# Joined input loads, sixteen rows of batch 5 loaded apart, and wide fp32 idle products in a linear-attention and soft-MoE kernel

## The chip, the core and the metric

The kernel runs on one core of one Trainium2 chip. Five engines work at the same time, each through its own list of instructions: TensorE (PE; its weight loads are listed apart as PEld), VectorE (DVE), ScalarE (ACT), GpSimd (POOL) and SyncE (SP). Here SP only issues the transfers between HBM and SBUF, which 16 DMA engines carry out. The metric is the device time of one execution in microseconds (us).

## The reference

Linear attention over 8 batches and 8 heads of 576 tokens of 64 features is followed by a root-mean-square norm; the result, 4608 tokens of 512 features, goes through a soft mixture of 8 experts with 4 slots each:

```python
kv = einsum('bhsd,bhse->bhde', k, v)
out = einsum('bhsd,bhde->bhse', q, kv)
x = out / sqrt(mean(out * out) + 1e-6) * g_norm      # 4608 x 512
logits = x @ phi                                     # 4608 x 32
d = softmax of logits over the 4608 tokens
slot_input = d.T @ x                                 # 8 experts x 4 slots x 512
slot_out = relu(slot_input @ w1[e]) @ w2[e]          # w1 512 x 1024, w2 1024 x 512
c = softmax of logits over the 32 slots
result = c @ slot_out                                # 4608 x 512
```

All data is fp32.

## The kernel before

The 4608 tokens are 36 tiles T of 128 tokens. Nine tiles make two batches.

**Attention.** For each batch b the class `Kv` builds the products of k and v in PSUM, for 8 heads at once. `products` (L205) multiplies the first 512 tokens, in four blocks of 128 rows for each of four head groups. `borders` (L220) adds the last 64 tokens. They lie in `kv_rest`, for one half of the batch (`g`) and one `w` on partitions 0 to 63, for the other `w` on partitions 64 to 127; the two halves of the output (`i`) go to rows 0 to 63 and 64 to 127 of PSUM, so that the four products of a half each have a quarter of PE's array. Then ACT copies the result to SBUF (`kvT`, L229), and `slots` (L234, L236) transposes it and multiplies it by phi; ACT and DVE put the results into one of two block-diagonal operands `bd` (L240, L248, L250). `kv_steps` says before which tile the steps (0, 1 and 2) of a batch run.

**Tiles.** For each T, `products(T)` (L264, L273) multiplies q by `bd` into a PSUM tile `o`, of which there are two; ACT squares it and evicts it (L283, L290, L291), DVE sums the squares (L296), ACT and DVE make the root (L304 to L314), POOL scales (L345, L323), DVE makes logits (L358), and every six tiles a running maximum and PE's `group_sum` (L422) add to the slot inputs `acc`.

**Experts.** After the last tile, `expert_h(e)` (L637) multiplies slot inputs by w1 and `expert_y(e, hf)` (L655) by w2, for two halves hf of the output columns. Half 0 of experts 2 to 7 runs through units 2, 3 and 4 of w2, two experts in each unit; half 1 runs through units 5, 6 and 7. `gather` and `mix` (L671, L675, L677) finish a half, and `output` (L688, L696, L698) makes one twelfth of the result and, when a row of `OUT_ROWS` is complete, sends it (L702).

**Idle products.** `fill(n)` (L465) issues n bf16 matmuls of zeros, 512 columns wide, whose result nobody reads. `EARLY` sets how many stand ahead of the first products and behind each half of batch 0, `LATE_FILL` how many stand at five places between the last tile and the experts.

**Transfers.** All of them are issued by SP, in the program's order. A load whose home is still being read waits, and what is behind it in SP's list waits with it. `place` addresses a large SBUF arena in units of 256 columns, whose parts are used again and again: `KV_AT`, `Q_AT`, `W_AT` and `OUT_AT` say where. `W_ROWS` lists the loads of weights, each the parts of one row next to each other. `loads_behind` says behind which tile a load is issued. Before the change, w2's units 3 and 4 are two loads, the first issued behind `expert_h(0)`, the second behind `expert_h(1)`.

Of the kernel before, what the change touches and what calls it, by code (L numbers as in the profile page):

```python
# [8 lines left out]
F32 = mybir.dt.float32  # L9
# [5 lines left out]
P = 128  # L15
# [12 lines left out]
NX = 14  # L28
EARLY = (9, 1, 0)
LATE_FILL = (16, 3, 3, 1, 1)  # L30
TOK = 4608
# [6 lines left out]
W_AT = {  # L38
# [3 lines left out]
}  # L42
W_ROWS = (
    (("w1", 0, None), ("w2", 0, None)),
    (("w1", 1, None), ("w2", 1, None)),
    (("w1", 2, None), ("w1", 3, None)),
    (("w1", 4, None), ("w2", 2, 1)),
    (("w1", 5, None),),
    (("w1", 6, None),),
    (("w1", 7, None),),  # L50
    (("w2", 2, 0),),
    (("w2", 3, None),),
    (("w2", 4, None),),
    (("w2", 5, None),),
# [4 lines left out]
OUT_ROWS = ((0, 1), (2, 3), (4, 5), (6,), (7, 8), (9, 10, 11))  # L59
HEAD = 144  # L60
SCRATCH = 1024
EPS_RMS = 1e-6
# [7 lines left out]
@with_exitstack  # L70
def soft_moe_linear_attention(ctx: ExitStack, tc: tile.TileContext, first_in, head_in, t2_in, kv5_in, t3_in, w_in, out):


    nc = tc.nc
# [10 lines left out]
    def place(at, n):  # L85
        return arena[:, HEAD + at * KB : HEAD + at * KB + n]

    def load_head(u, lo, hi):
        at = (KV_AT[0], KV_AT[1], Q_AT[0], KV_AT[2], Q_AT[1], KV_AT[3])[u]
        nc.sync.dma_start(place(at, TOK)[:, lo:hi], head_in[u, :, lo:hi])  # L90

    def load_row(at, src):
        nc.sync.dma_start(place(at, src.shape[-1]), src)
# [4 lines left out]
    def kv_rest(b, g):  # L98
        return place(KV_AT[b], TOK)[:, g * 2304 + 2048 : g * 2304 + 2304]

    def q_main(b):
# [22 lines left out]
    def w_block(kind, u, i):  # L124
# [8 lines left out]
    load_head(2, 0, 2048)  # L133
    load_head(1, 0, 2304)
    load_head(1, 2304, TOK)
    load_head(2, 2048, TOK)
# [6 lines left out]
        18: lambda: load_w("w1", 0),  # L143
        21: lambda: load_w("w1", 1),
        26: lambda: load_w("w1", 2),
        27: lambda: load_w("w1", 4),
        31: lambda: load_w("w1", 5),
    }
# [5 lines left out]
    ones = const.tile([P, P], F32, name="ones")  # L154
# [11 lines left out]
    for i in range(2):  # L166
        lo = 64 * i
# [20 lines left out]
    class Kv:  # L188
# [24 lines left out]
        def borders(self, gs):  # L213

            for g in gs:
                half = kv_rest(self.b, g).rearrange("p (w n) -> p w n", w=2)
                for i in range(2):
                    for w in range(2):
                        lo, at = 64 * i, 64 * w
                        nc.tensor.matmul(  # L220
                            self.pkv[lo : lo + 64, w, g],
                            lhsT=half[at : at + 64, 1, lo : lo + 64],
                            rhs=half[at : at + 64, 0, lo : lo + 64],
                            start=False,
                            stop=g == gs[-1],
                        )
            n = len(gs)
            self.kvT = wk.tile([P, n, 2, D], F32, tag="kvT", name=f"kvT{self.b}_{gs[0]}", bufs=1)
            nc.scalar.copy(self.kvT, self.pkv[:, :, gs[0] : gs[0] + n].rearrange("p w g d -> p g w d"))  # L229
# [206 lines left out]
    kv_steps = {(b, i - 3): (i,) for b in range(2, B) for i in range(3)}  # L436
    kv_steps.update({(1, -2): (0, 1), (1, -1): (2,)})

    def kv_step(b, i):
        if i == 0:  # L440
            kvs[b] = Kv(b)
            kvs[b].products(0)
            kvs[b].products(1)
        elif i == 1:
            kvs[b].products(2)
            kvs[b].products(3)
            kvs[b].borders((0, 1))
        else:
            kvs[b].slots((0, 1))
# [9 lines left out]
    def fill(n, cols=256, home=None):  # L459
# [4 lines left out]
        for i in range(n):  # L464
# [6 lines left out]
            )  # L471

    fill(EARLY[0], cols=512)

    for g in range(2):
        kv = Kv(0, "o" if g else "kv", 2 if g else None)
        kv.products(2 * g)
        kv.products(2 * g + 1)
        kv.borders((g,))
        kv.slots((g,))  # L480
        fill(EARLY[1 + g], cols=512)
    load_head(5, 0, TOK)
    load_head(4, 2048, TOK)
    load_row(KV_AT[4], t2_in)
    load_row(KV_AT[5], kv5_in)
    T_at, diag_at, pb_at, d_at, sums_at = {}, {}, {}, {}, {}
    for T in range(NT - 2):
# [4 lines left out]
        s = ends.get(T - 1)  # L492
# [64 lines left out]
    for i in todo_sums:  # L557
        group_sum(*i)
    load_w("w1", 6)
    load_w("w1", 7)  # L560
    load_w("w2", 2, 0)
    fill(LATE_FILL[0], home=ps.tile([P, 512], F32, tag="m", name="fill"), cols=512)
    group_max_T(G)
# [141 lines left out]

    expert_h(0)
    load_w("w2", 3)
    expert_h(1)
    load_w("w2", 4)
    expert_y(0, 0)  # L710
# [38 lines left out]
def build_program():  # L749
# [3 lines left out]
    shapes = {  # L753
        "first": (P, HEAD + 2304), "head": (6, P, TOK), "t2": (P, 2 * TOK), "kv5": (P, TOK), "t3": (P, 3 * TOK),
        "w": (1, 2 * NE * P * UNIT),
# [62 lines left out]
```

## Time and profile before

| | us |
|---|---|
| time, median of 3 runs (lowest, highest) | 175.09 (174.84, 175.16) |
| the profiled execution's own time | 174.76 |
| its span, first to last instruction | 173.0 |
| PE busy | 150.3 |
| DVE busy | 89.1 |
| ACT busy | 86.4 |
| POOL busy | 57.2 |

The span leaves out 1.8 us of the execution's own time. The page says how long each engine was busy, what share of the span the DMA engines worked, and it follows back the chain of work that ended last. Times of instructions are counted from the start of the span. PE works on fp32 in two records for each matmul, so 16 matmuls appear as x32. Other views quoted below give instructions in order of time (start, length, engine, line, operation, count, and in brackets the idle time before), the busy time in stretches (length; busy time of PE, PEld, DVE, ACT and POOL, each with its count of instructions; the granted clock of PE; the busy share of the DMA engines; GB/s), and for transfers the line, size and time from issue to landing.

### The profile page before, as it was taken

How to read it: one execution, taken by the hardware profiler on the slowest of the kernel's cores; microseconds unless marked ns; L12 is line 12 of the kernel's file. 1: busy time of each engine (PE TensorE's matmuls, PEld its weight loads, DVE VectorE, ACT ScalarE, POOL GpSimd, SP SyncE). 2: the span in 40 equal slices, each digit the busy share in tenths (PEclk: the TensorE clock that was granted, in tenths of full speed). 3: DMA queues.
4: the chain of work that ended last, by engine and by line, in shares of the span. 5: the costliest groups of instructions: out<-in, count | busy, mean ns of one | idle time of the engine just before them, and what ended most of it. 6: DMA issues, size and time to landing. Idle time of an engine off the chain costs nothing.

```text
span 173.0 us, 4659 instructions
## 1 busy us (share of the span) xinstructions
PE 150.3 (87%) x1973; PEld 108.3 (63%) x1973; DVE 89.1 (51%) x184; ACT 86.4 (50%) x224; POOL 57.2 (33%) x68
## 2 busy tenths in 40 slices
PE   7788999999979899999999796989999899978500
PEld 2467978888769788888897583346666435433200
DVE  1111456566576656566664776842888433456600
ACT  2024586976947976878859465112222131315500
POOL 6000067636557753477563676600000000000000
PEclk9999999999999999999999999999999999999955
DMA  5999999999999998999999999999999999999994
GB/s 199 420 429 427 447 404 447 399 506 409 405 413 473 479 435 359 417 436 415 440 440 415 426 411 421 424 432 415 434 419 424 424 424 425 393 404 418 418 452 196
DMA packets 4628, 71.67 MB, mean 414 GB/s; under 512 B 512, under 2 KB 512, under 8 KB 640
## 3 DMA queue, kind: packets, MB, share of 16 engines
q1 hardware_dynamic: 4608, 71.38, 97.3%
q8 instruction: 15, 0.25, 0.6%
q14 instruction: 5, 0.04, 0.1%
HBM read 61.94 MB, written 9.44 MB: 413 GB/s over the span
## 4 chain that ended last, share of the span: by engine, by line
PE 54%; DVE 16%; ACT 12%; POOL 5%; issue 4%; DMA 3%; POOLq 1%; DVEq 0%; ACTq 0%
PE o L273 13%; PE pY L655 9%; PE ph L637 8%; PE kvp_kv L205 7%; PE po L688 6%; POOL part L345 4%; DVE logits L358 4%; DVE ms L296 4%; DMA arena<-in_first_dram 3%; PE pS L422 2%; ACT sq L283 2%; DVE arena L698 2%; ACT bd L240 2%; ACT xall L291 1%; ACT r L304 1%
## 5 line engine op out<-in xcount | busy, mean ns | idle before, releaser
L273 PE MATMUL o<-bd,arena 128*128 128x192 f32 x256 | 49.3, 336 | 1.6 <-ACT xall L291 0.6
L273 PEld LDWEIGHTS o<-bd,arena 128*128 128x128 f32 x256 | 41.0, 191 | 4.4 <-ACT xall L291 1.7
L345 POOL TENSOR_TENSOR part<-part,r 128x512 f32<-128x512 f32 x17 | 17.8, 1047 | 52.6 <-DVE r L314 52.6
L323 POOL TENSOR_TENSOR xall<-xall,r 128x512 f32<-128x512 f32 x34 | 34.7, 1043 | 0.0
L358 DVE TENSOR_REDUCE logits<-part 128x64 f32<-128x512 f32 (+1 forms) x18 | 18.3, 1014 | 16.5 <-POOL part L345 16.4
L296 DVE TENSOR_REDUCE ms<-sq 128x16 f32<-128x1024 f32 (+1 forms) x19 | 21.9, 1154 | 5.8 <-ACT sq L283 5.7
L283 ACT ACTIVATE sq<-o 128x512 f32<-128x512 f32 x36 | 21.4, 596 | 6.1 <-PE o L273 5.8
L291 ACT COPY xall<-o 128x512 f32<-128x512 f32 x34 | 20.7, 609 | 0.0
L205 PE MATMUL kvp_kv<-arena 128*64 128x64 f32 x480 | 17.9, 231 | 0.9 <-DMA arena<-in_first_dram 0.9
L205 PEld LDWEIGHTS kvp_kv<-arena 128*64 128x64 f32 x480 | 15.9, 144 | 4.3 <-issue 1.9
L696 ACT COPY arena<-po 128x768 f32<-128x768 f32 x12 | 9.3, 800 | 18.5 <-PE po L688 18.4
L698 DVE COPY arena<-po 128x768 f32<-128x768 f32 x12 | 11.3, 956 | 10.6 <-PE po L688 9.8
L655 PE MATMUL pY<-arena,xall 128*32 128x256 f32 x256 | 15.6, 382 | 0.5 <-DVE y L671 0.5
L688 PE MATMUL po<-logits,z 32*128 32x384 f32 x96 | 13.5, 525 | 2.1 <-DVE z L677 0.9
L637 PE MATMUL ph<-arena,sTe 128*32 128x256 f32 x224 | 12.7, 380 | 0.3 <-DVE sTe L584 0.3
L655 PEld LDWEIGHTS pY<-arena,xall 128*32 128x32 f32 x256 | 7.8, 110 | 7.8 <-issue 1.4
L290 ACT COPY part<-o 128x256 f32<-128x256 f32 x34 | 12.6, 372 | 0.0
L304 ACT ACTIVATE r<-ms,eps 128x16 f32<-128x16 f32 x17 | 5.2, 308 | 14.7 <-DVE ms L296 14.5
L422 PE MATMUL pS<-xall,d 128*32 128x129 f32 x288 | 10.8, 278 | 2.0 <-ACT d L410 2.0
L688 PEld LDWEIGHTS po<-logits,z 32*128 32x128 f32 x96 | 5.8, 183 | 8.9 <-ACT arena L696 5.0
L637 PEld LDWEIGHTS ph<-arena,sTe 128*32 128x32 f32 x224 | 7.2, 110 | 5.3 <-DVE sTe L584 0.7
L422 PEld LDWEIGHTS pS<-xall,d 128*32 128x32 f32 x288 | 7.1, 109 | 5.1 <-issue 4.2
(93 smaller groups left out, 143.9 us busy)
## 6 DMA issues: line engine op xcount, KB each, us to landing
arena<-in_w_dram SPq DMA_DIRECT2D x7, 2048.0 KB, 17.6
arena<-in_w_dram SPq DMA_DIRECT2D x3, 4096.0 KB, 22.9
arena<-in_t_dram SPq DMA_DIRECT2D x1, 6912.0 KB, 36.1
out_dram<-arena SPq DMA_DIRECT2D x4, 1536.0 KB, 7.2
arena<-in_head_dram SPq DMA_DIRECT2D x2, 2304.0 KB, 22.5
arena<-in_t_dram SPq DMA_DIRECT2D x1, 4608.0 KB, 35.3
arena<-in_head_dram SPq DMA_DIRECT2D x3, 1152.0 KB, 11.9
arena<-in_w_dram SPq DMA_DIRECT2D x1, 3072.0 KB, 26.0
```

Source lines behind the costliest of these rows:

```text
L205: nc.tensor.matmul(self.pkv[lo : lo + 64, w, g], lhsT=main[:, w, 1, c, lo : lo + 64], rhs=main[:, w, 0, c, lo : lo + 64], start=c == 0 and ...
L273: nc.tensor.matmul(o[:, r, :192], lhsT=q_main(2 * g + i)[:, r, at : at + P], rhs=bds[i][:, r], start=True, stop=True)
L283: nc.scalar.activation(sqs[s][:, T - starts[s]], o[:, :, 32:160], AF.Square, scale=0.125)
L291: nc.scalar.copy(xts[T % NX][:, :, :128], o[:, :, 32:160])
L296: nc.vector.tensor_reduce(out=mss[s], in_=sqs.pop(s).rearrange("p t j (w d) -> p (t j w) d", w=2), axis=AX.X, op=ALU.add)
L323: nc.gpsimd.tensor_tensor(out=x, in0=x, in1=r[:, i].rearrange("p (j w) -> p j w", w=2).unsqueeze(3).to_broadcast([P, 4, 2, D]), op=ALU.mult,)
L345: engine.tensor_tensor(out=part, in0=part, in1=rs_of[s].unsqueeze(3).to_broadcast([P, STAGES[s], H, NS]), op=ALU.mult)
L358: nc.vector.tensor_reduce(out=L[:, pos(starts[s]) : pos(starts[s]) + STAGES[s]], in_=parts.pop(s).rearrange("p t h n -> p t n h"), axis=AX ...
L422: nc.tensor.matmul(pS[32 * j : 32 * j + 32], lhsT=ds[G][:, i], rhs=x[:, j], start=i == 0, stop=i == GROUPS[G] - 1)
L637: nc.tensor.matmul(ph[32 * j : 32 * j + 32], lhsT=sTe[:, (4 * e + c) * NS : (4 * e + c + 1) * NS], rhs=w_block("w1", e, 4 * c + j), start= ...
L655: nc.tensor.matmul(pY[32 * j : 32 * j + 32, hf, :256], lhsT=hTs[e][:, c], rhs=w_block("w2", u, at + c), start=e == 0 and c < 4, stop=e == ...
L688: nc.tensor.matmul(po[:, u, : CT * NS].rearrange("p (g x) -> p g x", g=2), lhsT=z[lo : lo + 32, f * P : (f + 1) * P], rhs=cT[k][lo : lo + 32],
```

## The change

Four things change; the rest of the diff follows from them.

1. **Loads joined.** k and v of batch 1 come in one load in place of two, and all three steps of batch 1 now run before tile 3 (before: steps 0 and 1 before tile 2, step 2 before tile 3). In `W_ROWS`, half a unit of w2 (`("w2", 2, 0)`), w1 of expert 6 and w1 of expert 5 become one load of 5 MB, issued behind the last tile; w2's units 3 and 4 become one load of 4 MB, issued behind `expert_h(1)`. The first two rows of weights are paired otherwise, with the same sizes and places.
2. **Batch 5.** The last 64 tokens of half 1 of batch 5 no longer ride on that batch's load (each of its 128 rows is 256 columns, 1 KB, shorter). They come as 16 rows of 2048 columns, in four transfers of four rows (rows i, i+4, i+8, i+12), issued between the loads of batch 4 and batch 5. `borders` multiplies them in 16 products of 16 rows in place of 4 products of 64 rows. All 16 stand on partitions 0 to 15.
3. **Wide idle products.** `fill_wide(n)` issues n fp32 matmuls of ones, 128 by 512 columns. Two stand behind the bf16 ones at the start, one each ahead of batches 1 and 2, and four take the place of the 16 bf16 ones behind the last tile.
4. **bf16 idle products.** At the start there are 5 in place of 9, and one more stands between `borders` and `slots` of each half of batch 0.

```diff
-EARLY = (9, 1, 0)
-LATE_FILL = (16, 3, 3, 1, 1)
+EARLY = (5, 1, 0)
+WIDE = (2, 1, 1)
+LATE_FILL = (4, 3, 3, 1, 1)
...
-    (("w1", 5, None),),
-    (("w1", 6, None),),
+    (("w2", 2, 0), ("w1", 6, None), ("w1", 5, None)),
     (("w1", 7, None),),
-    (("w2", 2, 0),),
-    (("w2", 3, None),),
-    (("w2", 4, None),),
+    (("w2", 3, None), ("w2", 4, None)),
...
+    def rest_pieces(b, g, w, cols):
+        if (b, g) == APART:
+            t = place(APART_AT, 2048)[:APART_ROWS].rearrange("p (s w c n) -> p s w c n", w=2, c=2, n=128)
+            return [(t[:, s, w, 1, cols], t[:, s, w, 0, cols]) for s in range(64 // APART_ROWS)]
+        t = kv_rest(b, g)[64 * w : 64 * w + 64].rearrange("p (c n) -> p c n", c=2)
+        return [(t[:, 1, cols], t[:, 0, cols])]
...
-    load_head(1, 0, 2304)
-    load_head(1, 2304, TOK)
+    load_head(1, 0, TOK)
...
-        31: lambda: load_w("w1", 5),
...
+                        pieces = rest_pieces(self.b, g, w, slice(64 * i, 64 * i + 64))
+                        for n, (v, k) in enumerate(pieces):
+                            nc.tensor.matmul(
...
-    kv_steps.update({(1, -2): (0, 1), (1, -1): (2,)})
+    kv_steps[1, -1] = (0, 1, 2)
...
         if i == 0:
+            if b < 3:
+                fill_wide(WIDE[b])
...
+    def fill_wide(n):
+        t = ps.tile([P, 512], F32, tag="m", name="fill").rearrange("p (a n) -> p a n", n=P)
+        for i in range(n):
+            nc.tensor.matmul(t, lhsT=ones, rhs=ones.unsqueeze(1).to_broadcast([P, 4, P]), start=True, stop=True)
+
     fill(EARLY[0], cols=512)
+    fill_wide(WIDE[0])
...
         kv.borders((g,))
+        fill(1, cols=512)
         kv.slots((g,))
...
     load_row(KV_AT[4], t2_in)
+    rest = place(APART_AT, 2048)[:APART_ROWS]
+    for i in range(4):
+        nc.sync.dma_start(rest[i::4], rest_in[i::4])
     load_row(KV_AT[5], kv5_in)
...
-    load_w("w1", 6)
+    load_w("w2", 2, 0)
     load_w("w1", 7)
-    load_w("w2", 2, 0)
...
     expert_h(0)
+    expert_h(1)
     load_w("w2", 3)
-    expert_h(1)
-    load_w("w2", 4)
     expert_y(0, 0)
```

Three places show what stands where. The first is PE around batch 1, before the change: kvp_kv and kvp_o are the products of k and v, o the tiles, kvT and gphi the operands of `slots`.

```order
L205 MATMUL kvp_o<-arena 64x64 x16
L220 MATMUL kvp_o<-arena 64x64 x4
L234 MATMUL kvp_o<-ident,kvT_1_167 128x128
L236 MATMUL kvp_o<-gphi,kvT_1_167 128x128
L273 MATMUL o_179<-bd_93,arena 128x192 x4
L273 MATMUL o_189<-bd_93,arena 128x192 x4
L205 MATMUL kvp_kv<-arena 64x64 x32
L220 MATMUL kvp_kv<-arena 64x64 x8
L273 MATMUL o_242<-bd_93,arena 128x192 x4
L234 MATMUL kvp_kv<-ident,kvT_0_240 128x128 x2
L236 MATMUL kvp_kv<-gphi,kvT_0_240 128x128 x2
```

The same place after the change:

```order
L242 MATMUL kvp_o<-gphi,kvT_1_167 128x128
L279 MATMUL o_185<-bd_92,arena 128x192 x4
L279 MATMUL o_195<-bd_92,arena 128x192 x4
L279 MATMUL o_205<-bd_92,arena 128x192 x4
L484 MATMUL fill<-ones 128x512
L211 MATMUL kvp_kv<-arena 64x64 x32
L226 MATMUL kvp_kv<-arena 64x64 x8
L240 MATMUL kvp_kv<-ident,kvT_0_269 128x128 x2
L242 MATMUL kvp_kv<-gphi,kvT_0_269 128x128 x2
L279 MATMUL o_279<-bd_92,arena 128x192 x4
```

The third tile's products moved ahead of batch 1, a wide idle product stands between, and no tile stands any more between the borders of batch 1 and its slots.

The second place is PE around the borders of batch 5, before and after; pS is `group_sum`, pm the maximum.

```order
L422 MATMUL pS_743<-xall,d_712 32x129 x8
L205 MATMUL kvp_kv<-arena 64x64 x16
L220 MATMUL kvp_kv<-arena 64x64 x8
L273 MATMUL o_818<-bd_93,arena 128x192 x4
L386 MATMUL pm_831<-ident,top_780 128x128
```

```order
L428 MATMUL pS_753<-xall,d_722 32x129 x8
L211 MATMUL kvp_kv<-arena 64x64 x16
L226 MATMUL kvp_kv<-arena 64x64 x20
L279 MATMUL o_840<-bd_92,arena 128x192 x4
L392 MATMUL pm_853<-ident,top_790 128x128
```

Eight products became twenty, at the same place of the list.

The third place is SP's list of loads, from the load of batch 3 to the last load of weights, before and after; t is batch 4 with its q (first) and batches 6 and 7 with theirs (second), kv batch 5, w weights.

```order
L90 DMA arena<-in_head_dram 128x4608
L90 DMA arena<-in_head_dram 128x2560
L93 DMA arena<-in_t_dram 128x9216
L93 DMA arena<-in_kv_dram 128x4608
L93 DMA arena<-in_t_dram 128x13824
L122 DMA arena<-in_w_dram 128x8192 x3
L122 DMA arena<-in_w_dram 128x6144
L122 DMA arena<-in_w_dram 128x4096 x2
L122 DMA xall<-in_w_dram 128x4096
L122 DMA arena<-in_w_dram 128x2048
L122 DMA arena<-in_w_dram 128x4096 x5
```

```order
L91 DMA arena<-in_head_dram 128x4608
L91 DMA arena<-in_head_dram 128x2560
L94 DMA arena<-in_t_dram 128x9216
L502 DMA arena<-in_rest_dram 4x2048 x4
L94 DMA arena<-in_kv_dram 128x4352
L94 DMA arena<-in_t_dram 128x13824
L130 DMA arena<-in_w_dram 128x8192 x3
L130 DMA arena<-in_w_dram 128x6144
L130 DMA arena<-in_w_dram 128x10240
L130 DMA xall<-in_w_dram 128x4096
L130 DMA arena<-in_w_dram 128x8192
L130 DMA arena<-in_w_dram 128x4096 x3
```

Two loads of 4096 columns and the one of 2048 became one of 10240, two of the five behind it became one of 8192, and four small transfers stand ahead of batch 5.

More of the change, by code (lines that the diff above doesn't have):

```diff
@@ L38 @@
 W_AT = {
[1 row of a table removed]
[1 row of a table added]
     ("w1", 3): (16,), ("w1", 4): (104,), ("w1", 5): (56,), ("w1", 6): (40,), ("w1", 7): None,
[1 row of a table removed]
[1 row of a table added]
 }
 W_ROWS = (
-    (("w1", 0, None), ("w2", 0, None)),
-    (("w1", 1, None), ("w2", 1, None)),
+    (("w1", 0, None), ("w1", 1, None)),
+    (("w2", 0, None), ("w2", 1, None)),
     (("w1", 2, None), ("w1", 3, None)),
     (("w1", 4, None), ("w2", 2, 1)),
-    (("w1", 5, None),),
-    (("w1", 6, None),),
+    (("w2", 2, 0), ("w1", 6, None), ("w1", 5, None)),
     (("w1", 7, None),),
-    (("w2", 2, 0),),
-    (("w2", 3, None),),
-    (("w2", 4, None),),
+    (("w2", 3, None), ("w2", 4, None)),
     (("w2", 5, None),),
@@ L60 @@
 HEAD = 144
+APART = (5, 1)
+APART_AT = 144
+APART_ROWS = 16
 SCRATCH = 1024
@@ L70, in soft_moe_linear_attention @@
 @with_exitstack
-def soft_moe_linear_attention(ctx: ExitStack, tc: tile.TileContext, first_in, head_in, t2_in, kv5_in, t3_in, w_in, out):
+def soft_moe_linear_attention(ctx: ExitStack, tc: tile.TileContext, first_in, head_in, t2_in, kv5_in, rest_in, t3_in, w_in, out):
     nc = tc.nc
@@ L143, in soft_moe_linear_attention @@
         18: lambda: load_w("w1", 0),
-        21: lambda: load_w("w1", 1),
+        21: lambda: load_w("w2", 0),
         26: lambda: load_w("w1", 2),
         27: lambda: load_w("w1", 4),
-        31: lambda: load_w("w1", 5),
     }
@@ L215, in borders @@
             for g in gs:
-                half = kv_rest(self.b, g).rearrange("p (w n) -> p w n", w=2)
                 for i in range(2):
                     for w in range(2):
[L219 to L226, printed above, removed]
+                        pieces = rest_pieces(self.b, g, w, slice(64 * i, 64 * i + 64))
+                        for n, (v, k) in enumerate(pieces):
+                            nc.tensor.matmul(
+                                self.pkv[64 * i : 64 * i + 64, w, g],
+                                lhsT=v,
+                                rhs=k,
+                                start=False,
+                                stop=g == gs[-1] and n == len(pieces) - 1,
+                            )
             n = len(gs)
@@ L558, in soft_moe_linear_attention @@
         group_sum(*i)
-    load_w("w1", 6)
+    load_w("w2", 2, 0)
     load_w("w1", 7)
-    load_w("w2", 2, 0)
-    fill(LATE_FILL[0], home=ps.tile([P, 512], F32, tag="m", name="fill"), cols=512)
+    fill_wide(LATE_FILL[0])
     group_max_T(G)
@@ L753, in build_program @@
     shapes = {
-        "first": (P, HEAD + 2304), "head": (6, P, TOK), "t2": (P, 2 * TOK), "kv5": (P, TOK), "t3": (P, 3 * TOK),
+        "first": (P, HEAD + 2304), "head": (6, P, TOK), "t2": (P, 2 * TOK), "kv5": (P, TOK - 256), "rest": (APART_ROWS, 2048), "t3": (P, 3 * TOK),
         "w": (1, 2 * NE * P * UNIT),
@@ L796 @@
     rows = [np.concatenate([w[k] for k in row], axis=1).reshape(-1) for row in W_ROWS]
+    rest = kv[5][:, TOK - 256 :].reshape(2, 64 // APART_ROWS, APART_ROWS, 256).transpose(2, 1, 0, 3)
+    rest = rest.reshape(APART_ROWS, 2048)
     first = np.zeros((P, HEAD + 2304), np.float32)
@@ L803 @@
         "in_t2_dram": np.concatenate([kv[4], qm[2]], axis=1),
-        "in_kv5_dram": kv[5],
+        "in_kv5_dram": np.ascontiguousarray(kv[5][:, : TOK - 256]),
+        "in_rest_dram": np.ascontiguousarray(rest),
         "in_t3_dram": np.concatenate([kv[6], qm[3], kv[7]], axis=1),
```

4 rows, old and new, of the table W_AT are left out of this document.

## The prediction

> **What bounds the kernel now.** I read the page's slices and DMA queues first, then the chain of waits, then short stretches at the end.
>
> ```profile
> DMA  5999999999999998999999999999999999999994
> q1 hardware_dynamic: 4608, 71.38, 97.3%
> q8 instruction: 15, 0.25, 0.6%
> PE 54%; DVE 16%; ACT 12%; POOL 5%; issue 4%; DMA 3%; POOLq 1%; DVEq 0%; ACTq 0%
> ```
>
> The DMA engines work through nearly all of the span: 97.3% of 173.0 us for 71.38 MB is 168.3 us for the 4357 KB of each engine, 38.6 ns per KB. Yet the chain that ended last is compute, over half of it PE. So two bounds lie side by side, and the question is which one sets the last transfer. The busy share of the DMA engines near the end tells it (stretch; busy times; clock, DMA share, GB/s):
>
> ```profile
> 154.00:154.50 0.50, 0.20 (x1) 0.00 (x0) 0.50 (x1) 0.41 (x1) 0.00 (x0) 1.00 0.93 393
> 154.50:155.00 0.50, 0.00 (x0) 0.00 (x0) 0.46 (x2) 0.00 (x0) 0.00 (x0) 1.00 0.64 270
> 155.00:155.50 0.50, 0.40 (x4) 0.34 (x8) 0.00 (x0) 0.00 (x0) 0.00 (x0) 1.00 0.52 221
> 155.50:156.00 0.50, 0.50 (x10) 0.39 (x4) 0.00 (x0) 0.00 (x0) 0.00 (x0) 1.00 0.99 418
> ...
> 170.00:170.50 0.50, 0.00 (x0) 0.00 (x0) 0.00 (x0) 0.00 (x0) 0.00 (x0) 0.50 0.61 258
> ...
> 171.50:172.00 0.50, 0.00 (x0) 0.00 (x0) 0.00 (x0) 0.00 (x0) 0.00 (x0) 0.50 0.01 0
> ```
>
> SP's issues and, below, times from issue to landing, in the same order (weights, then two outputs):
>
> ```profile
> 120.23 0.33 SPq L122 DMA_DIRECT2D arena<-in_w_dram  x1
> 154.70 0.33 SPq L702 DMA_DIRECT2D out_dram<-arena  x1
> 163.54 0.33 SPq L702 DMA_DIRECT2D out_dram<-arena  x1
> ```
> ```profile
> arena<-in_w_dram SPq DMA_DIRECT2D x1, 2048.0 KB, 15.3
> out_dram<-arena SPq DMA_DIRECT2D x1, 1536.0 KB, 6.5
> out_dram<-arena SPq DMA_DIRECT2D x1, 2304.0 KB, 8.6
> ```
>
> At 155.0 half of the engines have nothing to do: they wait for the third output row, issued at 154.70, and start at about 155.6, 0.9 us behind the issue. From there 1536 + 768 + 1536 + 2304 = 6144 KB are left, 384 KB an engine, 14.8 us: these engines end at 170.4, where the share falls to 0.61. The other half was never dry and ends at 171.5; their last landing, at 163.54 + 8.6 = 172.1, closes the kernel. The lag from last packet to landing is about 0.5 us. So the waiting engines land at 170.9, and compute has **1.2 us** of room: whatever delays the third output row by less is hidden by the busier engines; what delays it by more is paid.
>
> **The change part by part, loads.** The last 256 columns of batch 5 are 8 KB for each engine, 8 x 38.6 ns = 0.3 us earlier for every later load, on engines that take none of the four small transfers. Four loads fewer are 512 packets fewer; no row prices a packet apart from its bytes, so between nothing and 0.4 us; I take 0.2, since the rows give whole transfers near their bytes' price. Together the queue is 0.5 us earlier by the time of w2. Of the small transfers the trace has no like. Spread over all engines they cost nothing net; on four engines, 4 x 8 KB each, 1.2 us there; on one, 128 KB, 4.9 us. I take four, one row of each transfer per engine, since a row was one packet in all others (4608 packets are the rows and completions of 32 transfers). Half of the engines have room for 1.2 us, as 0.52 shows; if the four are among the others, w2 comes later (a rival).
>
> [...]
>
> **The joined loads of weights.** The 5 MB load waits for what its two later parts waited for, and goes out about when the first of those did; the queue then still holds the load before it. The 4 MB load is what matters. Its second half landed at 120.23 + 15.3 = 135.5; joined, both land then, less 0.5: 135.0. Who reads the first half (PE in order of time, then waits; six experts' pY, the first of which stands in the chain below)?
>
> ```profile
> 132.07 5.55 PE L655 MATMUL pY<-arena,xall 128*32 128x256 f32 x96
> ```
> ```profile
> PEld pY L655 <- DMA arena<-in_w_dram: 0.5, 1, 0.5
> ```
>
> Six experts of x16, 0.86 us each, start at 132.07; unit 3 is needed by the third, at 133.8. It would wait until 135.1, 1.3 us, and the small wait that stood before unit 4 (0.1 us on PE itself) would go: **+1.2 us** for all output, if nothing else moved.
>
> **The borders of batch 5.** The chain of waits runs through this step:
>
> ```profile
> 17.25 2.03 PE kvp_kv L205 x64
> ...
> 22.55 0.25 ACT bd L240
> ...
> 23.75 0.60 ACT sq L283
> ...
> 64.43 1.08 PE kvp_kv L205 x32
> 65.52 0.39 PE kvp_kv L220 x16
> 65.91 1.50 PE o L273 x8
> 67.41 0.22 PE pm L386 x2
> 67.63 0.58 PE pS L422 x16
> 68.20 0.37 PE kvp_kv L234 x2
> 68.57 0.45 PE kvp_kv L236 x4
> ...
> 88.99 1.51 PE o L273 x8
> ...
> 90.53 0.60 ACT sq L283
> ...
> 116.51 3.66 PE ph L637 x64
> ...
> 120.17 0.86 PE pY L655 x16
> ```
>
> From 60.7 to 90.5 the chain is PE without a gap; nothing there hides PE work. The 8 products of L220 take 0.39 us because four, each on its quarter of the array, go side by side. In the new half, 16 products have the same 16 rows and, eight by eight, the same columns, so each waits for the one ahead. What a record costs alone no row shows for this shape. Where two go side by side (L205: 64 records in 2.03 us), a place in line is 0.063 us; 32 records one by one are 2.0 us, less half of 0.39: **+1.8 us**. Bounds: at L220's pace (0.39/16 = 0.024) 0.8 - 0.2 = +0.6; with the weight load not hidden, at L234's 0.185 a record, +5.7. I take 1.8, the row nearest in shape.
>
> Behind 90.5 the chain turns to ACT, DVE and POOL, all fed by PE, and so on to the experts: all of it moves by 1.8 us. The third expert then arrives at 133.8 + 1.8 = 135.6, after the joined load: **the two delays do not add**. The output stage moves by 1.8 less the 0.1 of the wait: 1.7 us.
>
> **The start.** PE and the load of batch 1's second part:
>
> ```profile
> 1.05 4.02 PE L465 MATMUL fill<-zeros 128*128 128x512 bf16 x9 [1.05 <-DVE zeros L157]
> 6.00 1.98 PE L205 MATMUL kvp_kv<-arena 128*64 128x64 f32 x32 [0.93 <-DMA arena<-in_first_dram]
> 13.65 0.90 PE L273 MATMUL o<-bd,arena 128*128 128x192 f32 x4
> 15.06 2.19 PE L273 MATMUL o<-bd,arena 128*128 128x192 f32 x12 [0.51 <-DVE bd L248]
> ```
> ```profile
> arena<-in_head_dram SPq DMA_DIRECT2D x1, 1152.0 KB, 15.3
> ```
> ```profile
> 2.77 0.44 SPq L90 DMA_DIRECT2D arena<-in_head_dram  x1
> ```
>
> Matmuls here take 1.98 us where the same 32 records later take 1.08: PE runs at half its later pace, though its granted clock reads 1.00. Five bf16 products (0.43 each at this pace) and two wide ones (1.7 each, from eight records of 192 columns in 1.5 us, doubled) end at 6.6 instead of 5.1, and no gap of 0.93 us stands before 6.00. Batch 1's products now wait for 2.77 + 15.3 = 18.1; 2.0 us of them, borders 0.4, copy 0.4, slots 0.8 and the copies to the square of tile 3 (22.55 to 23.75 before) 1.2 end at 22.9, against 23.75 before. So if tiles 0 to 2 are done by 18.1, the start loses nothing. For that PE must come to its later pace by about 10 us. I take it so, for the unbroken stretch from 1.05 to about 8 (6.00 + 1.98), where before it broke off at 5.1. If not, tile 2 ends near 18.8, and a wide product, the later first products and the tile buffer shared with kvp_o make the start up to **2 us** late; the gain the other way is bounded by the load, under 0.8. The wide product ahead of batch 2 lies on ACT's and DVE's time until 50. I take 0 for the start.
>
> [...]
>
> Behind the last tile nothing changes: eight records of 512 columns cost what 16 bf16 products did, and PE waits for the logits there.
>
> ```profile
> 107.25 3.63 PE L465 MATMUL fill<-zeros 128*128 128x512 bf16 x16
> 111.10 0.43 PE L388 MATMUL pm<-ident,logits 128*32 128x128 f32 x8 [0.22 <-DVE logits L371]
> ```
>
> **The sum.** The third output row goes out at 154.70 + 1.7 = 156.4; the queue, 0.5 us earlier, is dry on all engines by then. They start at 157.3 and take 14.8 us and 0.5 to land: 172.6 instead of 172.1, rounded **+0.4 us**, since the old share shows the same sum to be up to 0.1 long. The profiled execution would be 175.2 (174.76 before, 0.33 under the median), the median **175.5 us**.
>
> **The rivals.** *A, the borders are cheap* (up to +1.3 of the bounds): then the joined 4 MB load decides, the output moves by 1.2 us, exactly the room: 175.1, no change. For it: L220's own pace. *B, faster:* the third row moves by less than 0.7 us, because the loads come a full microsecond earlier or PE makes up time after 138; the queue's 0.5 us then count: 174.6. Against it: PE has nothing to wait for between 138 and 154 that could give way. *C, the four rows fall on busy engines:* w2's 4 MB land 0.7 us later than before, at 136.2, the third expert waits until 136.3, the output moves by 2.4 us: 172.1 + 1.2, so 176.3. *D, the start stays slow, or weight loads are not hidden in the borders:* 2 to 4 us more on the chain, 177.5 or above.
>
> **How the numbers follow.** Forecast 0.44, A 0.25, B 0.10, C 0.10, D 0.11. The range takes in B and C and leaves out D and the far end: 174.5 to 176.5; the forecast's own is 175.2 to 175.9. A measurement of this kernel tells 0.2%, 0.35 us, from no change. The forecast is slower by more than that in some 0.65 of its cases, C and D always: 0.29 + 0.21 = 0.50. Faster is B and a little of A: 0.13. The rest, 0.37, is the same.
>
> **What would show it.** The borders of batch 5 near 65 us should take about 2.2 us; first PE products of the experts should start 1.8 us later than 116.5 us; PE should not wait for the joined load; the DMA share should fall well under 0.5 before the third output row. If the borders take under 1 us and PE stands at the third expert until 135, it is A; if w2 lands after 136, C; if matmuls at 13 us still run at half pace, D. I am wrong in the main step if the third row goes out before 155.9.

## The result and the profile after

The median is 178.12 us (177.94 to 178.38, six executions) against 174.97 us before (174.84 to 175.16) on the same chip: slower by the ratio 1.0181, 95% interval 1.0168 to 1.0194. That is 3.15 us, and outside the predicted range of 174.5 to 176.5 us. The profiled executions took 177.94 and 174.76 us, 3.18 us apart. Here and below, an execution more than 1.5% above the fastest of its kernel is left out (one each of noapart, before_apart and start_old).

The page after: PE's busy time with its records (weight loads beside it), the slices of DMA, and the DMA queues.

```profile
PE 153.2 (87%) x1995; PEld 109.6 (62%) x1995; DVE 89.1 (51%) x184; ACT 86.5 (49%) x224; POOL 57.2 (32%) x68
DMA  5999999999999998999999998998999999889993
q1 hardware_dynamic: 4064, 71.38, 95.8%
q8 instruction: 16, 0.26, 0.6%
```

The bytes are the same, but the DMA row has eights near 107 and 121 us and between 150 and 159, where before there were nines. PE has 1995 records in place of 1973, and instructions were fetched 16 times in place of 15. The page of before has for the same rows:

```profile
PE 150.3 (87%) x1973; PEld 108.3 (63%) x1973; DVE 89.1 (51%) x184; ACT 86.4 (50%) x224; POOL 57.2 (33%) x68
```

The chain of waits after, at the borders of batch 5, the first expert, and the experts that read the joined load:

```profile
64.74 1.08 PE kvp_kv L211 x32
65.82 2.10 PE kvp_kv L226 x40
...
118.49 3.71 PE ph L654 x64
...
137.02 3.69 PE pY L672 x64
```

Against 65.52 and 116.51 before, PE is 0.30 us late as it reaches the borders and 1.98 us late at the first expert: the borders take 2.10 us in place of 0.39. PE in order of time shows the next loss (the bracket is idle time and what the profile names as its end):

```profile
134.06 1.91 PE L672 MATMUL pY<-arena,xall 128*32 128x256 f32 x32
137.02 3.66 PE L672 MATMUL pY<-arena,xall 128*32 128x256 f32 x64 [1.05 <-DVE xall L666]
```

Two experts run, then PE stands 1.05 us at the third. The DVE transpose that this expert needs had ended at 132.26, 4.8 us before; the trace's landings (16 increments of the semaphore for a load of 128 rows, taken as one from each of the 16 DMA engines) put the 4 MB load at 134.77 on the fastest engine and 136.88 on the slowest, 0.14 us ahead of PE's start. So the wait is for the DMA. SP's issues, and the busy share of the DMA engines around the 5 MB load (after first, then before; the last three columns are clock, DMA share, GB/s):

```profile
106.12 0.33 SPq L130 DMA_DIRECT2D arena<-in_w_dram  x1
122.21 0.33 SPq L130 DMA_DIRECT2D arena<-in_w_dram  x1
157.76 0.33 SPq L719 DMA_DIRECT2D out_dram<-arena  x1
166.59 0.33 SPq L719 DMA_DIRECT2D out_dram<-arena  x1
```
```profile
105.50:106.00 0.50, 0.50 (x4) 0.30 (x2) 0.27 (x1) 0.20 (x1) 0.06 (x1) 1.00 0.64 246
106.00:106.50 0.50, 0.09 (x1) 0.00 (x0) 0.11 (x1) 0.47 (x3) 0.00 (x0) 1.00 0.23 98
106.50:107.00 0.50, 0.00 (x0) 0.00 (x0) 0.43 (x4) 0.34 (x1) 0.00 (x0) 1.00 0.12 49
```
```profile
106.50:107.00 0.50, 0.50 (x28) 0.50 (x20) 0.40 (x4) 0.35 (x1) 0.50 (x1) 1.00 1.08 459
```

The load ahead of it (3 MB) landed between 105.03 and 108.45. The 5 MB load went out at 106.12, when the first engines had been done for a microsecond, and its first packet started at 107.08. In between the engines stood dry one after the other. Behind it, the fastest engine had the 4 MB 2.5 us later than before (134.77 against 132.27, where unit 4 landed) and the slowest 1.3 us later (136.88 against 135.55).

The third output row went out at 157.76 in place of 154.70: 3.06 us = 0.30 + 1.71 + 1.05. The last transfer, issued at 166.59, shows the end:

```profile
out_dram<-arena SPq DMA_DIRECT2D x1, 2304.0 KB, 8.7
```
```profile
173.00:173.50 0.50, 0.00 (x0) 0.00 (x0) 0.00 (x0) 0.00 (x0) 0.00 (x0) 0.50 0.01 0
174.00:174.50 0.50, 0.00 (x0) 0.00 (x0) 0.00 (x0) 0.00 (x0) 0.00 (x0) 0.50 0.09 37
```

Fifteen engines had landed by 174.02, the fastest at 173.77. One landed at 175.33: after 173.5 the only data packets left are two of 18 KB, one behind the other, on a single engine. A 16 KB fetch of instructions began at 164.46 and took 0.94 us, in the middle of the output. Before, no fetch fell behind 149.6.

### The profile page after: what moved, and what is told of

It reads as the page before. It is cut to its first block, busy times and chain, and to the rows that moved or that the text cites. A ratio compares the mean times of both kernels' runs of the same rounds, so it can differ in the third digit from the quotient of the medians.

```text
span 176.2 us, 4695 instructions
## 1 busy us (share of the span) xinstructions
PE 153.2 (87%) x1995; PEld 109.6 (62%) x1995; DVE 89.1 (51%) x184; ACT 86.5 (49%) x224; POOL 57.2 (32%) x68
## 4 chain that ended last, share of the span: by engine, by line
PE 53%; DVE 15%; ACT 11%; DMA 9%; issue 3%; POOL 2%; SPq 1%; POOLq 0%; DVEq 0%
PE o L279 17%; DMA arena<-in_head_dram 9%; PE kvp_kv L211 9%; PE pY L672 6%; PE po L705 6%; PE pS L428 3%; PE fill L484 3%; PE kvp_kv L226 3%; PE ph L654 2%; DVE arena L715 2%; PE o L270 2%; DVE logits L364 2%; POOL part L351 2%; ACT bd L246 1%; ACT arena L713 1%
## 5 line engine op out<-in xcount | busy, mean ns | idle before, releaser
L211 PEld LDWEIGHTS kvp_kv<-arena 128*64 128x64 f32 x480 | 15.1, 138 | 5.7 <-DMA arena<-in_head_dram 2.3
L211 PE MATMUL kvp_kv<-arena 128*64 128x64 f32 x480 | 17.1, 225 | 0.7 <-DMA arena<-in_head_dram 0.7
```

What stands on the lines that cost most here:

```text
L211: nc.tensor.matmul(self.pkv[lo : lo + 64, w, g], lhsT=main[:, w, 1, c, lo : lo + 64], rhs=main[:, w, 0, c, lo : lo + 64], start=c == 0 and ...
```

## The experiments

The theories: **1**, two delays in a row (the late PE makes the joined load late, which makes PE later); **2**, the late PE alone, the late load being hidden; **3**, the joined transfers are slow in themselves. **4** and **5** came up on the way: a longer list of PE instructions adds a fetch; the 5 MB join costs time even where PE is not late. The table has them all. Records, fetches, the issue of the third output row, and the landings of the last transfer on the fastest and the slowest engine are those of the one profiled execution, whose own time stands beside the median.

| kernel | PE records | fetches | third row out | last landing | its time | median (range) |
|---|---|---|---|---|---|---|
| before | 1973 | 15 | 154.70 | 170.7 / 172.1 | 174.76 | 174.97 (174.84 to 175.16) |
| after | 1995 | 16 | 157.76 | 173.8 / 175.3 | 177.94 | 178.12 (177.94 to 178.38) |
| split5 | 1995 | 16 | 156.74 | 172.7 / 174.3 | 177.16 | 177.16 (176.85 to 177.28) |
| split4 | 1995 | 16 | 156.58 | 172.6 / 174.4 | 177.18 | 177.14 (177.07 to 177.47) |
| noapart | 1971 | 15 | 159.35 | 175.4 / 175.5 | 178.41 | 177.02 (175.84 to 178.41) |
| before_apart | 1997 | 16 | 156.41 | 172.4 / 174.4 | 177.24 | 177.25 (177.12 to 178.63) |
| interleaved | 1995 | 16 | 156.96 | 173.0 / 174.5 | 177.14 | 177.43 (177.14 to 177.81) |
| before_more | 1997 | 16 | 156.33 | 172.3 / 174.5 | 177.07 | 175.74 (175.54 to 177.42) |
| apart32 | 1973 | 15 | 156.03 | 172.0 / 173.9 | 176.66 | 177.18 (176.66 to 177.41) |
| start_old | 1989 | 15, and one behind the landing | 157.60 | 173.6 / 173.8 | 177.66 | 176.90 (176.34 to 178.23) |
| join4 | 1973 | 15 | 156.46 | 172.5 / 173.0 | 175.71 | 175.66 (175.26 to 176.53) |
| join5 | 1973 | 15 | 156.13 | 172.1 / 173.9 | 176.65 | 176.45 (175.91 to 177.99) |
| start_new | 1971 | 15 | 155.37 | 171.4 / 172.3 | 175.01 | 174.97 (174.76 to 175.16) |
| apart32_nojoin | 1973 | 15 | 155.09 | 171.1 / 172.3 | 175.20 | 175.37 (175.02 to 175.62) |

Beside the other kernels the median of before lay between 174.97 and 175.11. The ratios take in all executions of before, some of which (three of 11 beside split5, four of 33 beside join4) took 175.6 to 176.3 us, and so do not follow the medians exactly. One regularity holds in every row: the fastest engine lands 16.0 us behind the issue of the third row. What differs is how far the slowest engine is behind it: 0.2 to 2.1 us.

**split5.** The three loads of before.

```diff
-    (("w2", 2, 0), ("w1", 6, None), ("w1", 5, None)),
-    (("w1", 7, None),),
+    (("w1", 5, None),),
+    (("w1", 6, None),),
+    (("w1", 7, None),),
+    (("w2", 2, 0),),
...
+        31: lambda: load_w("w1", 5),
...
-    load_w("w2", 2, 0)
+    load_w("w1", 6)
     load_w("w1", 7)
+    load_w("w2", 2, 0)
```

> After, but the 5 MB load of weights is three loads again, w1 of expert 5 issued behind tile 31 as before. Theory 1 (two delays in a row): the borders and the start make PE 2.0 us late; so the joined 5 MB load goes out at 106.1 in place of 104.1, when the first DMA engines have already finished what was queued at 105.0; they stand dry, w2's 4 MB land at 136.9, and PE stands 1.05 us at the third expert. Here the queue is never dry, the 4 MB land at about 135.5, PE stands under 0.3 us there, the third output row goes out at 156.7 to 157.0 (after: 157.8), and the time is about 177.0. Theory 2 (the 2.0 us alone set the time, the late load is hidden): 178.1, as after. Theory 3 (the joined transfers are slow in themselves, whenever they are issued): the 4 MB still land past 136.5 and the time is over 177.6.

The ratio to before is 1.0102 (1.0076 to 1.0128), the time 177.16. PE stood 0.44 us in place of 1.05, since the 4 MB landed at 133.6 to 135.87. The third row came 1.02 us earlier than in after: 0.61 of it is the shorter stand, and 0.40 is a PE that was earlier at the first expert already (118.09 against 118.49). Theory 2, which had 178.1, is out. The 4 MB, too, were issued too late here: at 121.81, 0.32 us before the fastest engines were done at 122.13, so that they were 1.3 us later than in before (133.6 against 132.27).

**split4.** Units 3 and 4 in two loads.

```diff
-    (("w2", 3, None), ("w2", 4, None)),
+    (("w2", 3, None),),
+    (("w2", 4, None),),
...
     expert_h(0)
-    expert_h(1)
     load_w("w2", 3)
+    expert_h(1)
+    load_w("w2", 4)
```

> After, but w2's units 3 and 4 are two loads again, one behind each of the first two experts. Theory 1: the DMA engines still stand dry near 106, but unit 3 lands by about 134.5, before the third expert needs it at 136.0; PE doesn't stand there, and the time is about 177.0. Theory 2: 178.1. Theory 3: 177.0 as well.

Ratio 1.0106 (1.0081 to 1.0132), 177.14. Unit 3 landed by 131.8, unit 4 by 136.7, and the experts run through, at the same start as in after:

```profile
134.06 5.44 PE L673 MATMUL pY<-arena,xall 128*32 128x256 f32 x96
```

With DVE as late as in after, PE does not stand: it was the load that it stood for. The third row came 1.18 us earlier than in after; the medians differ by 0.98 us.

**noapart.** The last tokens of batch 5 in its own load again.

```diff
-APART = (5, 1)
+APART = None
...
-    rest = place(APART_AT, 2048)[:APART_ROWS]
-    for i in range(4):
-        nc.sync.dma_start(rest[i::4], rest_in[i::4])
     load_row(KV_AT[5], kv5_in)
```

> After, but the last tokens of batch 5 come with that batch's load again, in 4 products of 64 rows. Theory 1: PE is 0.3 us late at 65 in place of 2.0; the 5 MB load goes out at 104.4, the first engines are dry for under 1 us, the 4 MB land at 135.2 to 135.7, PE stands 1.0 to 1.4 us at the third expert (needed at 134.3), the third row goes out at about 156.1, the time is 176.2 to 176.5. Theory 2: the borders were the cost, 175.3. Theory 3: the 4 MB land at 136.9 as in after, PE stands 2.6 us, and the time is 177.6 or more.

Here theory 1 missed and theory 3 was nearer: the load went out at 104.43, as expected, and yet the 4 MB landed at 133.4 to 136.78. The times scatter, from 175.84 to 178.41. The profile shows why a little lateness can cost much (PE, then the stretches, with the granted clock third from the end):

```profile
136.92 5.35 PE L669 MATMUL pY<-arena,xall 128*32 128x256 f32 x64 [2.63 <-DMA arena<-in_w_dram]
```
```profile
137.00:138.00 1.00, 1.00 (x20) 0.70 (x23) 0.00 (x0) 0.00 (x0) 0.00 (x0) 0.97 1.04 442
138.00:139.00 1.00, 1.00 (x16) 0.64 (x11) 0.00 (x0) 0.00 (x0) 0.00 (x0) 0.50 0.88 377
140.00:141.00 1.00, 1.00 (x15) 0.57 (x11) 0.00 (x0) 0.00 (x0) 0.00 (x0) 0.50 1.04 442
```

PE stood 2.63 us, and then its granted clock fell to 0.50 for some 3 us: the same 64 records took 5.35 us in place of 3.66. The third row is late by 0.3 + 2.63 + 1.69 = 4.6 us. In after PE was 1.7 us later at this point, so that it stood for 1.05 us only and kept its clock (1.00 from 137 to 140). The median of this kernel is no measure of the borders.

**before_apart.** Before, with the small transfers and the 16 products alone (the first two rows of weights paired as in after).

```diff
+APART = (5, 1)
...
+    rest = place(APART_AT, 2048)[:APART_ROWS]
+    for i in range(4):
+        nc.sync.dma_start(rest[i::4], rest_in[i::4])
     load_row(KV_AT[5], kv5_in)
```

> Before, with the last tokens of batch 5 loaded apart and nothing else (the first two rows of weights are paired as in after). All theories: borders of batch 5 2.1 us in place of 0.39, the output stage 1.7 us late, the third row out at 156.4. What differs is how much of it is hidden by the DMA engines that are behind the others: by the prediction's room of 1.2 us the time is 175.5; if that room is not there, since the engines that were behind are no longer so when all of them run dry, and a fetch of instructions can fall on any of them, it is 176.7.

The third row went out at 156.41, as expected, with the borders in the chain again at

```profile
65.60 2.10 PE kvp_kv L230 x40
```

The ratio is 1.0138 (1.0098 to 1.0178); three of five executions lie at 177.1 to 177.3, two above. That is more than even the sum without room, 176.7: fifteen engines landed by 172.6, only 0.4 us behind the last of before, as the prediction had it for a third row at 156.4; but one landed at 174.35, and again a fetch had fallen into the output, at 163.49. The kernels with 1995 or 1997 records have it, those with 1971 or 1973 do not. Hence theory 4.

**interleaved.** The order of the 16 products.

```diff
-                for i in range(2):
-                    for w in range(2):
-                        pieces = rest_pieces(self.b, g, w, slice(64 * i, 64 * i + 64))
-                        for n, (v, k) in enumerate(pieces):
+                for n in range(64 // APART_ROWS if (self.b, g) == APART else 1):
+                    for j in range(4):
+                            w, i = divmod(j, 2) if (self.b, g) == APART else (j % 2, j // 2)
+                            pieces = rest_pieces(self.b, g, w, slice(64 * i, 64 * i + 64))
+                            v, k = pieces[n]
```

> After, with the 16 products of batch 5's last tokens in another order: the two halves of the output columns take turns, where in after eight products with the same columns follow each other. Theory 1a: a product waits for the one ahead because both use the same columns; taking turns, two run side by side, the borders take 1.1 to 1.2 us in place of 2.10, PE is 0.9 us earlier, the 5 MB load goes out at 105.2, and the third output row goes out 0.4 to 0.9 us earlier than at 157.76 (the 4 MB load still ends last at the third expert): 177.2 to 177.7. Theory 1b: they wait because they share the 16 rows of the array; the order changes nothing: 2.1 us, 178.1.

```profile
65.81 1.35 PE kvp_kv L227 x40
```

1.35 us in place of 2.10: theory 1a in kind, 0.2 us short of its number. The single records of after bear it out: neighbours with the same columns start 0.06 us apart, also where the next product goes to another piece of PSUM, and only around the one change of columns do two start 0.01 us apart; so it is the columns that neighbours wait for, and not the sum in PSUM. The 32 records on 16 rows took (2.10 - 0.2) / 32 = 0.059 us each one behind the other, and (1.35 - 0.2) / 32 = 0.036 taking turns. The third row came 0.80 us earlier than in after, the time is 177.43, ratio 1.0136 (1.0120 to 1.0152).

**before_more.** Nothing but a longer list of PE instructions.

```diff
     for k, f in chunks:
         output(1, k, f)
+    for _ in range(12):
+        nc.tensor.matmul(pY[:, 0, :256], lhsT=ident, rhs=ones.unsqueeze(1).to_broadcast([P, 2, P]), start=True, stop=True)
```

> Before, with 12 fp32 idle products (24 records, as many as the 12 further products of batch 5 give) at the very end of PE's list, behind the last product of the output, where nobody waits for them. Theory 4 (length of PE's list): the kernels with 1971 and 1973 PE records fetched instructions 15 times, those with 1995 and 1997 did it 16 times, the last at 163.4 to 164.5, and that fetch holds one DMA engine for about 1.0 us amid the output; here a 16th fetch appears near 160, and where it falls on an engine that was behind already the last landing comes at up to 173.5 in place of 172.1: executions between 175.0 and 176.4. Rival: the 16th fetch belongs to the four small transfers or to a longer run: 15 fetches and 175.0.

```profile
PE 154.7 (88%) x1997; PEld 111.9 (64%) x1997; DVE 89.1 (51%) x184; ACT 86.5 (49%) x224; POOL 57.2 (33%) x68
q8 instruction: 16, 0.26, 0.6%
```

The 16th fetch is there, and five of nine executions lie between 175.54 and 175.74. The medians are 0.7 us apart (175.74 against 175.03), for products that nobody waits for; the ratio, 1.0068 (1.0040 to 1.0096), counts four later executions as well. The profiled execution is one of these, with PE 1.6 us late at batch 5 already; in it the fetch came at 167.19, the idle products ended at 169.47, ahead of the first landing at 172.34, and one engine landed 1.9 us behind the other fifteen. So theory 4 holds for the fetch; that the fetch makes the 0.7 us was not seen in an execution of the five. The other traces agree with its price: with a fetch in the output and no other engine late (after, split5, before_apart, interleaved, before_more) one engine lands 1.3 to 1.9 us behind the next, and without one, where all engines had run dry (noapart, start_old), all land within 0.2 us. Why that is more than the fetch's own 0.9 to 1.1 us is open.

**apart32.** The change with four edits.

```diff
-WIDE = (2, 1, 1)
+WIDE = (2, 0, 0)
...
-    (("w2", 3, None), ("w2", 4, None)),
+    (("w2", 3, None),),
+    (("w2", 4, None),),
...
-APART_ROWS = 16
+APART_ROWS = 32
...
-        fill(1, cols=512)
         kv.slots((g,))
```

> After, with four edits: w2's units 3 and 4 loaded apart; batch 5's last tokens as 32 rows, 8 products in place of 16, in four transfers of eight rows; no wide product ahead of batches 1 and 2; no bf16 one behind batch 0's borders. PE's list has 1973 records again, as before. By theories 1 and 4 the borders take 1.15 to 1.2 us, PE is 0.8 to 1.0 us late at the experts and doesn't stand at the third, the third row goes out at 155.5 to 155.8, there is no 16th fetch, the engines that run dry land last at 171.6 to 171.9 and the others near 172.3: 175.0 to 175.5. If the 16th fetch has nothing to do with the length of PE's list, it is there as well and the time is 176.0 to 176.7.

The borders took 1.17 us and no fetch fell into the output, as expected. The time was missed by 1.7 us: 177.18 (ratio 1.0125, 1.0109 to 1.0140). PE stood after all, 0.77 us, at the fifth expert:

```profile
137.03 1.93 PE L672 MATMUL pY<-arena,xall 128*32 128x256 f32 x32 [0.77 <-DMA arena<-in_w_dram]
```

Unit 4 landed at 133.47 to 136.89, 1.2 to 1.3 us later than before, though PE was hardly late and the 5 MB load went out at 104.60. So this load costs time without the borders, too: theory 5.

**start_old.** After with the start of before.

```diff
-EARLY = (5, 1, 0)
-WIDE = (2, 1, 1)
+EARLY = (9, 1, 0)
...
-    load_head(1, 0, TOK)
+    load_head(1, 0, 2304)
+    load_head(1, 2304, TOK)
...
-    kv_steps[1, -1] = (0, 1, 2)
+    kv_steps.update({(1, -2): (0, 1), (1, -1): (2,)})
```

(The wide products of the start and the bf16 one ahead of `slots` are gone as well.)

> After, with the start as before: nine bf16 idle products and no wide ones there, batch 1's k and v in two loads and its steps before tiles 2 and 3. Theory 1: PE is 0.3 us earlier at 65, all that follows too; the 5 MB load goes out at 105.8, the 4 MB land 0.3 us earlier than at 136.9: third row at 157.4, 177.8. Rival: the wide products gain, since matmuls run at their later pace from 6.5 us on, and without them PE is later at 65 than 65.8 by up to 1 us: 178.5 to 179.

The borders began at 65.77, against 65.82 in after: the 0.30 us by which after is behind before at that place can't be put down to the start; executions with the start of before began them between 65.52 and 67.23 (before_more). But this list has 1989 records, and its 16th fetch came at 176.96, behind the last landing. The pair shows what the fetch costs. The last transfer went out at 166.44 here and 166.59 in after, and took, from issue to landing,

```profile
out_dram<-arena SPq DMA_DIRECT2D x1, 2304.0 KB, 7.4
```

in place of 8.7: all 16 engines landed between 173.61 and 173.79, where in after one came 1.3 us behind the rest. The execution's own time did not gain as much: it lies 2.9 us above its span, where in the other profiled executions it is 1.8 to 1.9. Why the executions of start_old range from 176.34 to 178.23 is open.

**join4.** Before, with the 4 MB load alone.

```diff
-    (("w2", 3, None),),
-    (("w2", 4, None),),
+    (("w2", 3, None), ("w2", 4, None)),
...
     expert_h(0)
-    load_w("w2", 3)
     expert_h(1)
-    load_w("w2", 4)
+    load_w("w2", 3)
```

(Here, in join5 and in start_new the first two rows of weights are paired, and unit 4 is placed, as in after.)

> Before, with w2's units 3 and 4 in one load behind the second expert, and nothing else. Issued at 120.23 as unit 4 was, 2.3 us before the first DMA engines finish what is queued (122.5), so no engine stands dry; unit 3 lands with unit 4 at about 135.5. The third expert needs it at 133.8: PE stands 1.7 us, the third output row goes out at 156.3, the engines that wait for it land last at 172.4: 175.1 to 175.5. If the queue comes out 0.5 us earlier, as the prediction had it: landing 135.0, third row 155.9, 175.0 to 175.2.

175.66, ratio 1.0030 (1.0007 to 1.0053), 0.2 us above what was expected; the load landed at 133.2 to 135.59. In the profiled execution PE was 1.5 us late before it came there, and stood 0.28 us only; no trace shows what the join costs an execution whose PE is as early as in before.

**join5.** Before, with the 5 MB load alone.

```diff
-    (("w1", 5, None),),
-    (("w1", 6, None),),
+    (("w2", 2, 0), ("w1", 6, None), ("w1", 5, None)),
     (("w1", 7, None),),
-    (("w2", 2, 0),),
...
-        31: lambda: load_w("w1", 5),
```

> Before, with half a unit of w2, w1 of expert 6 and w1 of expert 5 in one 5 MB load behind the last tile, and nothing else. Theory 5 (the join alone makes the queue late, without a late PE): it goes out at 104.1 in place of 89.1, 1.2 us before the first engines finish at 105.3; they start at about 105.2 to 105.5 with a first packet 0.6 us longer than the others, so all later loads land 0.6 to 1.3 us later; unit 4 lands at 136.2 to 136.8, the fifth expert (135.5) stands 0.7 to 1.2 us, the third row goes out at 155.4 to 155.9, the engines that never wait land last at 172.7 to 173.3: 175.5 to 176.2. Rival (without the borders' delay the join costs nothing): unit 4 at 135.5, 175.0.

176.45, ratio 1.0081 (1.0049 to 1.0113). Unit 4 landed at 133.6 to 136.99, PE stood 0.91 us at the fifth expert, the third row went out at 156.13. Theory 5 holds: the join costs about 1.4 us with nothing else changed.

**start_new.** After without the borders' change and without the two joins of weights; what is left is the start, batch 1's joined load and the wide products.

> After without the borders' change and without the two joined loads of weights: the new start, batch 1's joined load, the wide products. 1971 PE records. If the start costs 0.3 us on PE, as the chains of before and after show at 65 us, and there is 1.2 us of room: third row at 155.0, 175.0. If there is no room: 175.3.

174.97, ratio 0.9986 (0.9968 to 1.0004): no difference. The third row went out at 155.37, 0.67 us later than before, and the last landing came at 172.33, 0.19 us later. The room is real.

**apart32_nojoin.** apart32 with the 5 MB load in three again, as in split5.

> The kernel of 32 rows (8 products, 1973 PE records), with the 5 MB load in three loads again too. The 5 MB join was what still made unit 4 late there (136.89, PE 0.77 us). Theory 5: here unit 4 lands by 135.9, PE doesn't stand, the third row goes out at 155.1 to 155.4, all engines land by 172.1 to 172.5: 175.0 to 175.4. Rival (the small transfers make the slowest engines late): unit 4 past 136.5 and 176 or more.

175.37, ratio 1.0005 (0.9986 to 1.0023). PE did not stand, unit 4 landed at 135.81, the third row went out at 155.09. Without joins and without a longer list the tokens come apart with no gain and next to no cost: the interval holds no change, the median lies 0.37 us above that of before (175.00). No kernel here beat before.

## Why the prediction was wrong, point by point

**The bounds: right.** Two bounds side by side, and the wait of the third output row as what decides. The engines that wait land 16.0 us behind its issue in all kernels; the prediction had 0.9 + 14.8 + 0.5 = 16.2. start_new shows 0.67 us hidden by the room.

**The queue 0.5 us earlier: not seen.** The first row of weights landed at 78.30 on the fastest engine and 80.67 on the slowest, against 78.59 and 80.36: the gain is there on the fastest only. The 0.2 us for 512 fewer packets was the author's estimate, and no run shows it apart. The four small transfers have one early increment each and four more, 0.31 us apart from one transfer to the next (47.26, 47.57, 47.89 and 48.20 for the first of the four), and of the 464 packets under 512 B on the page of after, 16 for each of the other 28 transfers (before: 512 for 32) leave 16, four for each small one: they lie on four engines and cost these 1.25 us, as the sum had it; which four they are the trace doesn't show. That they are four of those with room fits the landings of the first row of weights: before, nine engines had it by 79.76 and seven from 80.21 on; after, five by 78.71 and eleven from 79.46 on.

**The borders +1.8: right**, 1.71 us, for the reason given: before, four records of L220 start within 0.02 us and the next four 0.06 us behind the first of them; after, most of the 32 start singly, 0.06 us apart; interleaved, where neighbours no longer share their columns, gave 0.75 of it back.

**The start 0: right, but not by the reason given.** PE was 0.30 us late at 65.82, no more than executions differ there, and matmuls ran at their later pace from 6.5 us on (1.15 us for the 32 records that took 1.98). But the old start does that as well: in join4, with nine bf16 products that end at 5.08 and a gap behind them,

```profile
6.30 1.15 PE L214 MATMUL kvp_kv<-arena 128*64 128x64 f32 x32 [1.22 <-DMA arena<-in_first_dram]
```

and the same 1.15 us stand in before_apart, before_more, join5 and start_old. So the half pace in the trace of before is not the old start's doing, and no unbroken stretch was needed; that one raises the pace was the author's assumption, and no run sets it apart. The 0 came out right in part by luck. (The clock's records begin where the pace rises: at 13.82 in before, 6.31 in after, 3.8 to 5.2 in those five; the 1.00 that the prediction read ahead of it is the absence of a record.) In the same paragraph a wide product at half pace should be 2.0 us by the row quoted, not 1.7; the sum does not use it.

**The 5 MB load "goes out about when the first of those did; the queue then still holds the load before it": this is the step that failed.** Before, that issue (104.11) stood 1.2 us ahead of the first engines' end (105.33), and what bridged the place was the load of expert 5's w1, issued at 89.06, which the join took back to the last tile. The prediction moved all compute by 1.8 us and forgot that this load's issue is released by compute: it moved to 106.12, and the queue ran dry. Even unmoved (join5) it came too late for a smooth passage.

**"The two delays do not add": wrong, by the same step.** The 4 MB landed by 136.88 in place of 135.0, and PE, 2.0 us late, stood 1.05 us all the same. split4 gives all of it back, split5 0.61 us.

**Missing: the 16th fetch.** The sum looked at what 12 more products cost PE, and not at PE's list as a load of its own. By the 16.0 us of the table the engines land at 173.8 in after, 1.7 us behind the end of before; the fetch puts one of them at 175.33. The difference of 3.18 us between the profiled executions is so 3.06 us by which the third row is late, less the 1.4 us of room between the fastest and the slowest engine of before, plus 1.5 us for the one engine with the fetch. Against the prediction's own sum (175.2 for the profiled execution) 2.74 us are missing: 0.30 by which PE came late to batch 5, 1.05 of PE standing, and 1.5 of the fetch, less the 0.2 us by which 16.2 was long.

**The rivals.** C's effect came (the 4 MB late, PE standing at the third expert), but not from its cause, four rows on busy engines: with the same rows and no join (before_apart) unit 4 landed by 135.37, no later than before. D's start did not happen. A fell with the borders at 2.10 us.

## What to carry to other kernels

A joined load goes out when the last of its homes is free (after: the 5 MB load at 106.12; before: expert 5's w1 alone at 89.06), and its readers wait for its slowest engine (after: the 4 MB load landed from 134.77 to 136.88, and PE went on at 137.02); where the queue is to stay full, subtract from the lead of each issue whatever else in the change delays the engine that releases it, before two delays are called parallel. Where transfers set the end, a handful of further instructions on a long list can add a fetch that takes a DMA engine out in the worst place (24 further PE records in before_more came with a 16th fetch; in after the 16th took 0.94 us, amid the output): compare the fetches on the page and when the last of them falls. And a stand of some 2 us can cost PE more than itself, if its clock falls behind it (noapart: 2.63 us, and 1.69 us more at a clock of 0.50).

## What the runs showed of the hardware that was not expected

- **Fetches.** 16 KB each, one at a time, 0.9 to 1.1 us. Fifteen up to the last landing with at most 1989 PE records, sixteen with 1995. At which place of PE's list the 16th comes is not shown.
- **The clock.** After a stand of 2.63 us (noapart) the granted clock was 0.50 for 3.4 us. In the profiled execution of join4, whose start is that of before, PE stood 1.97 us for batch 1 and then ran at half pace:

```profile
19.00:20.00 1.00, 1.00 (x25) 0.77 (x21) 0.00 (x0) 0.00 (x0) 0.00 (x0) 0.50 1.27 541
21.00:22.00 1.00, 1.00 (x4) 1.00 (x4) 0.50 (x3) 0.00 (x0) 0.28 (x1) 0.50 1.12 479
```

  It reached the borders of batch 5 at 66.98 in place of 65.52. In before_more the clock fell in the same way behind 2.35 us. Length alone does not decide: stands of 2.48 us (start_old) and 2.60 us (join5) at the same place left the clock at 1.00, and so did the 1.05 us of after. With the new start PE stood at most 1.33 us for batch 1 in all eight traces and kept its clock there, and the 12 executions of start_new lie within 0.4 us of each other, where those of before beside them reach 176.3. That the one makes the other is not shown.
- **A queue that has run dry.** From the issue at 106.12 to the first packet 0.96 us passed, and the first 40 KB packet took 1.9 to 2.7 us on 13 of the 16 engines, where most later ones took 1.51 to 1.53.
